# A recurrent layer and a mixture of experts in one pass: visits planned anew, kept rows written later

## The chip, the cores and the metric

The kernel runs on one core of a Trainium2 chip. The metric is the device time of one execution in microseconds, as the median of several runs; lower is better. The engines are PE (matrix multiply), DVE (vector), ACT (scalar), POOL (GpSimd) and SP (sync, which here only reads a few registers and issues transfers).

## The reference

`x` and `f_logit` are 4 x 5056 x 256. A gated recurrence runs over the 5056 steps, and its output passes through a layer of 8 experts, of which each token uses at most one.

```python
def _attn_ref(x, f_logit, lower_bound):
    sig = 1.0 / (1.0 + np.exp(-f_logit))
    f = lower_bound[None, None, :] + (1.0 - lower_bound[None, None, :]) * sig
    i = 1.0 - f
    for t in range(S):
        h = f[:, t] * h + i[:, t] * x[:, t]
        y[:, t] = h
...
def _moe_ref(x, w_skip, w_gate, w1, w2):        # x: 20224 x 256
    do_compute = x @ w_skip > 0
    out = x.copy()
    xc = x[do_compute]
    logits = xc @ w_gate
    e_idx = np.argmax(logits, axis=1)
    ...
    gate_w = probs[np.arange(len(xc)), e_idx]
    for e in range(E):                           # E = 8, hidden width 1024
        mask = e_idx == e
        h = np.maximum(xc[mask] @ w1[e], 0.0)
        y[mask] = gate_w[mask, None] * (h @ w2[e])
    out[do_compute] = xc + y
```

On the reference's inputs 9914 of the 20224 tokens are computed, between 937 and 1630 for each expert; the others keep the recurrence's output.

## The kernel before

The sequence is cut into 21 **chunks**: two of 128 steps, eighteen of 256, one of 192, each for all four batches, so a full chunk has 1024 tokens, eight tiles of 128. A chunk goes through these steps:

- `load_z`, `load_x`: two transfers of 1 MB, issued by ACT (`zt` has two buffers, `xt` three).
- `tanh`, `affine` on ACT, `mixin`, `carry_in` and four `scan` on DVE: the recurrence.
- `turn_out`: for each tile PE transposes the states and computes the nine scores; ACT's `evict` brings them to `rows` (three buffers).
- `route0` to `route3`, `exps`, `gates`: on DVE mostly, with two small matmuls: the expert of each token and its place in a table in memory, ordered by expert.
- `send`: one indirect transfer per tile on POOL writes the token's row to its place in that table (`dispatched`).
- `keep`: one transfer of 1 MB, issued by ACT, writes the recurrence's rows to the output.

A **visit** takes `ns` tiles of one expert's part of the table through both matrix products. `window` (DVE) computes from the counts of chunk `m` which rows it takes; if too few are there, it reaches back over rows that were done, and masks these. `fetch` (SP) reads the rows once all sends of chunks up to `m` have landed. `load_w` (SP) brings the weights in four pieces of 512 KB; each is split into a high half on ACT (`split_hi`) and a low one on DVE (`split_lo`). `turn_in` transposes the rows on PE, `x_hi` and `x_lo` split them. Then come eight blocks of the hidden width (in four steps for `ns` = 2): `first` (three products of halves for each of two depths), `rect_hi` on ACT, `rect_lo` on DVE, `second`. `weigh` (DVE) multiplies by the gate and `put_out` (POOL, one indirect transfer per tile) writes the rows over the kept ones; for that it needs the kept rows of all chunks up to `m`.

`VISITS` lists the fixed visits as (expert, tiles, m). What is left of each expert afterwards is listed on the chip itself, after the last chunk is routed: `list1` to `list4` (some fifty small DVE operations, four transposes and two matmuls) cut the rest into visits of two and three tiles, and the listed visits read their expert and place from that list. `SURE` says how many of these are written out in the program, of two tiles and of three; a loop at the end would run any others.

The **order** of all instructions on each engine is written out before the program is built. Each step is a job with an engine, an estimated cost, a due time and the jobs and buffers that it needs; a greedy simulation gives each engine, whenever it is free, the startable job with the earliest due time. On the chip each engine runs its instructions in that order, and waits on semaphores for what an instruction really needs. A need that stands only in the plan moves an instruction's place in the queue and adds no wait of its own.

Due times come from `begin`, the nominal start of each visit, counted from `T0` = 57 with 5.76 us a tile and 0.47 us a `turn_out`; `ready` of a chunk is the begin of the first visit that needs it, less `FETCH`. A chunk's loads are due at `ready` - 46, its scans at - 24, its sends at - 11, its `keep` at + 4. Fetch and window of a visit are due at its begin - `FETCH`, its weight loads 16 before their use.

Of the kernel before, what the change touches and what calls it, by code (L numbers as in the profile page):

```python
# [36 lines left out]
RW = D + 2  # L37
EW = 2 * E1 + D

T0, FETCH, LAG = 57.0, 22.0, 3  # L40
LOWR = 80

VISITS = [(3, 2, 3), (1, 3, 4), (2, 3, 5), (5, 3, 7), (6, 4, 8), (0, 4, 10), (4, 4, 12), (7, 4, 13), (1, 4, 15),
          (3, 4, 17), (5, 4, 18)]
SURE = ((0, 16), (1, 3))


def tiles_of(c):
    return CHUNKS[c][1] * B // P
# [25 lines left out]
class Plan:  # L75
# [6 lines left out]
    def job(self, eng, cost, due, fn, *args, need=(), takes=(), uses=(), kb=0, lands=2.8):  # L82
        j = Job(eng, cost, due, fn, args, [n for n in need if n is not None], list(takes), kb, lands, len(self.jobs))
        for s_ in list(takes) + list(uses):
            s_.users.append(j)
        self.jobs.append(j)
        return j
# [67 lines left out]
def hgrn_moe(ctx, tc, z_d, x_d, lb_d, wr_d, w1_d, w2_d, out_d, disp_d):  # L155
# [9 lines left out]
    job = plan.job  # L165
# [44 lines left out]
    for nt in sorted({tiles_of(c) for c in range(NCH)}):  # L210
        r = cp.tile([P, E1, nt], F32, name=f"reset{nt}")
# [168 lines left out]
    W1S, W2S = [P, KD, F // 2], [P, NFB // 2, D]  # L380
    NV = len(VISITS)
    mask_all = cp.tile([P, NV, MS], I32, name="mask_all")
    offi_all = cp.tile([P, NV], I32, name="offi_all")
    visits = [dict(e=e, ns=ns, i=i, m=m, w={}, raw={}, hid={}) for i, (e, ns, m) in enumerate(VISITS)]

# [156 lines left out]
    def list2():  # L542
# [6 lines left out]
        for w, (num, frm) in enumerate(tl_["nums"]):  # L549
# [3 lines left out]
            le = new(f"left{w}", [P, 1])  # L553
            V.tensor_scalar(out=le, in0=inc[:, E - 1:E], scalar1=float(-SURE[w][1]), scalar2=0.0,
                            op0=ALU.add, op1=ALU.max)
# [47 lines left out]
    def tail_visit(w, i):  # L603
        ns = 2 + w
        v = dict(ns=ns, tail=True, m=NCH - 1, w={}, raw={}, hid={})

        def mask():
            mk = sb.tile([P, MS], I32, name="mk", bufs=3)
            lim = sb.tile([P, 1], F32, name="lim", bufs=3)
            V.tensor_copy(lim, limr[:, w, bass.ds(i, 1)])  # L610
            V.tensor_scalar(out=mk[:, :ns], in0=seqf[ns], scalar1=lim, scalar2=float(-BIG),
                            op0=ALU.subtract, op1=ALU.mult)
            v["mk"] = mk[:, :ns]

        v["mask"] = mask
        v["off"] = lambda: SP.value_load(lrow[0:1, 2 * w, bass.ds(i, 1)], min_val=0, max_val=ROWS - ns * P)
        v["ereg"] = lambda: SP.value_load(lrow[0:1, 2 * w + 1, bass.ds(i, 1)], min_val=0, max_val=E - 1)
        return v

    sure = [(0, i) for i in range(SURE[0][1])]  # L620
    for i in range(SURE[1][1]):
        sure.insert((i + 1) * len(sure) // (SURE[1][1] + 1), (1, i))
    visits += [tail_visit(w, i) for w, i in sure]
# [6 lines left out]
    PE_TILE, PE_TURN, DVE_CHUNK = 5.76, 0.47, 11.0  # L630
    begin, t, last = [], T0, VISITS[0][2]
    for v in visits:
# [19 lines left out]
    J = {}  # L652
    J["clear"] = job("SP", 1.3, ready[0], clear, kb=660)
    for c in range(NCH):
        nt, r = tiles_of(c), ready[c]
        cols = CHUNKS[c][1] * B
        f = cols / (B * TC)
        s_z, s_x, s_r = new_slot("zt"), new_slot("xt"), new_slot("rows")
        st[c].update(s_x=s_x)
        lz = job("ACT", .66, r - 46, load_z, c, takes=[s_z], kb=cols)  # L660
        lx = job("ACT", .66, r - 45.5, load_x, c, takes=[s_x], kb=cols)
        mix = []
        for k in range(KD):
            t_ = job("ACT", .17 + .86 * f, r - 29 + 2 * k, tanh, c, k, need=[lz], uses=[s_z])
            a_ = job("ACT", .33 + .86 * f, r - 28 + 2 * k, affine, c, k, need=[t_], uses=[s_z])
            mix.append(job("DVE", .13 + 1.08 * f, r - 26 + k, mixin, c, k, need=[a_, lx], uses=[s_z, s_x]))
        ci = job("DVE", .5, r - 24.5, carry_in, c, need=mix + J.get(("scan", c - 1), []),
                 uses=[s_z, s_x] + ([st[c - 1]["s_x"]] if c else []))
        sc = [job("DVE", .06 + 1.08 * f, r - 24 + i, scan, c, i, need=[ci], uses=[s_z, s_x]) for i in range(4)]
        J["scan", c] = sc  # L670
        ev = []
        for j in range(nt):
            s_p = new_slot("pt")
            half = 2 * (j >= nt // 2)
            to = job("PE", PE_TURN, r - 20 + j * 5 / nt, turn_out, c, j, need=sc[half:half + 2], takes=[s_p], uses=[s_x])
            ev.append(job("ACT", .31, r - 19.8 + j * 5 / nt, evict, c, j, need=[to],
                          takes=[s_r] if j == 0 else [], uses=[s_p] + ([s_r] if j else [])))
        J["keep", c] = job("ACT", .62, r + 4, keep, c, need=ev, uses=[s_r], kb=cols)
        r0 = job("DVE", .62, r - 14, route0, c, need=ev + [J.get(("gates", c - 1))], uses=[s_r])
        xp = job("ACT", .25, r - 14, exps, c, need=[r0])  # L680
        r1 = job("DVE", 1.2, r - 14, route1, c, need=[r0])
        s_p, s_o = new_slot("pt"), new_slot("posi")
        r2 = job("PE", .06, r - 13.5, route2, c, need=[r1], takes=[s_p])
        r3 = J["route3", c] = job("DVE", 1.1, r - 13, route3, c, need=[r2], takes=[s_o], uses=[s_p])
        ga = J["gates", c] = job("DVE", .55, r - 13, gates, c, need=[xp, r3], uses=[s_r])
        J["send", c] = [job("POOL", 1.28, r - 11 + j * 1.2, send, c, j, need=[r3, ga], uses=[s_r, s_o], kb=129, lands=4.0)
                        for j in range(nt)]

    l1 = job("DVE", 2.7, begin[len(VISITS)] - FETCH - 12, list1, need=[J["route3", NCH - 1]])
    l2 = job("DVE", 7.0, begin[len(VISITS)] - FETCH - 11, list2, need=[l1])  # L690
    s_p, s_q = new_slot("pt"), new_slot("pt")
    l3 = job("PE", .9, begin[len(VISITS)] - FETCH - 8, list3, need=[l2], takes=[s_p, s_q])
    l4 = job("DVE", 1.0, begin[len(VISITS)] - FETCH - 7, list4, need=[l3], uses=[s_p, s_q])
    win = None
    split_of, fetched = {}, None
    for v, t in zip(visits, begin):
# [10 lines left out]
        else:  # L707
# [5 lines left out]
                           kb=ns * 129, lands=4.5)  # L713
# [14 lines left out]
        for k in range(KD):  # L728
# [3 lines left out]
                     uses=[s_p] + ([s_xh] if k else []))  # L732
            xr.append(job("DVE", .1 + .52 * w, t - 3, x_lo, v, k, need=[xh], takes=[s_xl] if k == 0 else [],
                          uses=[s_p, s_xh] + ([s_xl] if k else [])))
        s_po = [new_slot("po") for _ in range((ns + 1) // 2)]
        sec = None
        for u in range(n):
# [4 lines left out]
                     uses=[s_xh, s_xl] + ws[h, "w1"][1])  # L742
            hi = job("ACT", .1 + .43 * w * nb, tu + .5 * step, rect_hi, v, u, need=[f1], takes=[s_hh], uses=[s_ph])
            lo = job("DVE", .09 + .52 * w * nb, tu + .6 * step, rect_lo, v, u, need=[hi], takes=[s_hl],
                     uses=[s_ph, s_hh])
# [5 lines left out]
        for s_ in range(ns):  # L751
            ob = job("DVE", .42, end - 1, weigh, v, s_, need=[sec, po], takes=[s_ob] if s_ == 0 else [],
                     uses=[s_po[s_ // 2], s_in] + ([s_ob] if s_ else []))
            job("POOL", 1.36, end + 1 + s_, put_out, v, s_, need=[ob] + [J["keep", c] for c in range(m + 1)],
                uses=[s_ob, s_in], kb=128)
# [6 lines left out]
    with tc.If(more > 0):  # L762
        for w in range(2):
            cnt = nc.values_load(Tn[0:1, 1 + w:2 + w], min_val=0, max_val=P)
            with tc.If(cnt > SURE[w][1]):
                with tc.For_i(SURE[w][1], cnt, 1) as ri:
                    v = tail_visit(w, ri)
# [61 lines left out]
```

## Time and profile before

| | |
|---|---|
| median of 3 runs | 658.42 us (656.15 to 659.28) |
| the profiled execution | 660.33 us |
| its span, first to last instruction | 658.6 us |
| mean granted PE clock | 0.936 |
| first matmul of a visit | 97.0 us |
| last matmul of a visit | 651.1 us |

The profile shows one execution. Its times run from the first instruction, in us unless marked ns. "PEclk" is the share of its clock that PE was granted. "A<-B" behind an idle time names what ended it. In a group, the numbers behind the bar are the busy time and the mean duration of one; a tile name without its number stands for all its buffers. PE's matmuls are pipelined, so their rows overlap, and the step from one start to the next is the better price.

### The profile page before, as it was taken

To read this page: it belongs to the slowest core of one execution; us is meant where nothing else is said; L and a number is where in the kernel's file an instruction comes from. 1 tells how busy PE (TensorE), PEld (TensorE's weight loads), DVE (VectorE), ACT (ScalarE), POOL (GpSimd) and SP (SyncE) were. 2 spreads that over 40 slices of the span, in tenths; PEclk is the share of its full clock that TensorE was granted. 3 is DMA by queue.
4 is the path that set the end of the run, shared out by engine and by line. 5 is a ranking of instruction groups with operands and counts; after the bars stand their busy time and mean duration, and the time that the engine had idled before them with its cause. 6 is when DMAs were issued, how large, how long until landed. Compare 5 with 4: busy or idle time off the path is not lost. (4 is left out here: it accounts for less than half of the span.)

```text
span 658.6 us, 12335 instructions
## 1 busy us (share of the span) xinstructions
PE 585.1 (89%) x4202; PEld 555.3 (84%) x4202; DVE 531.4 (81%) x1190; ACT 379.9 (58%) x616; POOL 294.0 (45%) x271
## 2 busy tenths in 40 slices
PE   3356449999999998999999979999999999999995
PEld 3255449998989897979897969999999999999995
DVE  6878788999999997999999686877688677867762
ACT  4564557866776757567665415565556555545540
POOL 1427772685748745867756750411131122111212
PEclk9566669999999997999999979999999999999999
DMA  8989885988978877989756437676567558656710
GB/s 295 417 281 293 289 288 202 302 261 310 339 267 283 312 251 260 320 281 313 274 177 229 140 103 267 204 256 223 164 204 232 171 169 276 208 176 198 246 60 31
DMA packets 61413, 157.59 MB, mean 239 GB/s; under 512 B 9577, under 2 KB 30849, under 8 KB 56736
## 3 DMA queue, kind: packets, MB, share of 16 engines
q1 hardware_dynamic: 22544, 74.16, 35.0%
q10 hardware_dynamic: 27376, 62.13, 27.7%
q0 software_dynamic: 11424, 20.44, 8.5%
q8 instruction: 35, 0.57, 0.4%
q14 instruction: 34, 0.28, 0.1%
HBM read 114.91 MB, written 52.73 MB: 255 GB/s over the span
## 5 line engine op out<-in xcount | busy, mean ns | idle before, releaser
L374 POOL DMA_INDIRECT dispatched<-rows,posi x158 | 202.0, 1279 | 101.2 <-issue 27.7
L514 POOL DMA_INDIRECT out<-ob,xin x80 | 88.7, 1109 | 254.3 <-DVE ob L510 208.3
L481 ACT ACTIVATE hh<-ph 128x512 fp32r<-128x512 f32 (+1 forms) x172 | 97.5, 567 | 161.6 <-PE ph L474 158.5
L503 PE MATMUL po<-w2h,hh 128*128 128x256 f32 x640 | 185.6, 290 | 0.0
L503 PE MATMUL po<-w2h,hl 128*128 128x256 f32 x640 | 180.1, 281 | 0.0
L503 PE MATMUL po<-w2l,hh 128*128 128x256 f32 x640 | 180.0, 281 | 0.0
L488 DVE SCALAR_TENSOR_TENSOR hl<-ph,hh 128x512 fp32r<-128x512 f32 (+1 forms) x172 | 110.9, 647 | 61.2 <-ACT hh L481 60.7
L474 PE MATMUL ph<-xh,w1h 128*128 128x256 f32 (+2 forms) x480 | 157.0, 327 | 0.0
L474 PE MATMUL ph<-xl,w1h 128*128 128x256 f32 (+2 forms) x480 | 154.8, 323 | 0.0
L474 PE MATMUL ph<-xh,w1l 128*128 128x256 f32 (+2 forms) x480 | 154.4, 322 | 0.0
L292 PE MATMUL pt<-rk,xt 128*128 128x137 f32 x632 | 110.6, 324 | 39.3 <-DVE xt L285 18.0
L292 PEld LDWEIGHTS pt<-rk,xt 128*128 128x128 f32 x632 | 98.4, 222 | 49.0 <-DVE xt L285 19.4
L503 PEld LDWEIGHTS po<-w2h,hl 128*128 128x128 f32 x640 | 121.2, 189 | 1.2
L503 PEld LDWEIGHTS po<-w2h,hh 128*128 128x128 f32 x640 | 120.8, 189 | 1.0
L503 PEld LDWEIGHTS po<-w2l,hh 128*128 128x128 f32 x640 | 121.0, 189 | 0.0
L474 PEld LDWEIGHTS ph<-xl,w1h 128*128 128x128 f32 x480 | 91.7, 191 | 5.1
L474 PEld LDWEIGHTS ph<-xh,w1h 128*128 128x128 f32 x480 | 92.1, 192 | 3.3
L474 PEld LDWEIGHTS ph<-xh,w1l 128*128 128x128 f32 x480 | 91.8, 191 | 3.4
L285 DVE TENSOR_TENSOR_SCAN xt<-zt,xt 128x512 f32<-128x512 f32 (+2 forms) x84 | 93.6, 1146 | 0.2
L298 ACT ACTIVATE rows<-pt 128x274 f32<-128x274 f32 x158 | 62.2, 398 | 48.6 <-PE pt L292 43.2
L431 DVE TENSOR_TENSOR w1l<-rw,w1h 128x1024 fp32r<-128x1024 f32 x60 | 73.2, 1220 | 10.1 <-ACT w1h L426 9.7
L431 DVE TENSOR_TENSOR w2l<-rw,w2h 128x1024 fp32r<-128x1024 f32 x60 | 73.2, 1220 | 7.9 <-ACT w2h L426 7.9
(116 smaller groups left out, 541.5 us busy)
## 6 DMA issues: line engine op xcount, KB each, us to landing
rw<-w SPq DMA_DIRECT2D x120, 512.0 KB, 4.6
xt<-x ACTq DMA_DIRECT2D x18, 1024.0 KB, 7.2
zt<-z ACTq DMA_DIRECT2D x18, 1024.0 KB, 8.2
out<-rows ACTq DMA_DIRECT2D x18, 1024.0 KB, 9.1
xin<-dispatched SPq DMA_DIRECT2D x17, 258.0 KB, 3.8
xin<-dispatched SPq DMA_DIRECT2D x7, 516.0 KB, 3.6
dispatched<-rows,posi POOLq DMA_INDIRECT x158, 5.0
xin<-dispatched SPq DMA_DIRECT2D x6, 387.0 KB, 5.3
```

Source lines behind the costliest of these rows:

```text
L285: V.tensor_tensor_scan(out=xt[:, k, sl], data0=zt[:, k, sl], data1=xt[:, k, sl], initial=0.0, op0=ALU.mult, op1=ALU.subtract)
L292: T.matmul(pt[:, k * (E1 + P):(k + 1) * (E1 + P)], xt[:, k, cs], rk[k], start=True, stop=True)
L298: A.activation(st[c]["rows"][:, j], st[c]["pt", j], AF.Copy)
L374: si = G.indirect_dma_start(out=disp_d, out_offset=bass.IndirectOffsetOnAxis(ap=posi[:, j:j + 1], axis=0), in_=rows[:, j, E1:E1 + RW], in_ ...
L431: V.tensor_tensor(out=lo, in0=v["raw"][h, nm], in1=v["w"][nm, h][0], op=ALU.subtract)
L474: T.matmul(ph[:, i], a[:, k, cs], b[:, k, :w], start=(n == 0), stop=(n == 5))
L481: A.activation(th, v["hid"][u], AF.Relu)
L488: V.scalar_tensor_tensor(out=tl, in0=ph, scalar=0.0, in1=th, op0=ALU.max, op1=ALU.subtract)
L503: T.matmul(po, a[:, i, cs], b[:, c], start=(fb == 0 and n == 0 and s % 2 == 0), stop=(fb == NFB - 1 and n == 2), skip_group_check=True)
L514: oi = G.indirect_dma_start(out=out_d, out_offset=bass.IndirectOffsetOnAxis(ap=v["ids"][:, s, D:D + 1], axis=0), in_=v["ob"][:, s], in_off ...
```

## The change

The list of fixed visits is new: 20 instead of 11, with 70 tiles instead of 39. The first four have two tiles and ask for one chunk more each; then, with two exceptions of three tiles, all have four. The last four ask for the last chunk. The listed visits written out go from 16 of two tiles and 3 of three to 2 and 2. `FETCH` goes from 22 to 30. In the plan, `keep` of a chunk needs the first scan of the chunk two later.

```diff
-T0, FETCH, LAG = 57.0, 22.0, 3
+T0, FETCH, LAG = 57.0, 30.0, 3
 LOWR = 80
 
-VISITS = [(3, 2, 3), (1, 3, 4), (2, 3, 5), (5, 3, 7), (6, 4, 8), (0, 4, 10), (4, 4, 12), (7, 4, 13), (1, 4, 15),
-          (3, 4, 17), (5, 4, 18)]
-SURE = ((0, 16), (1, 3))
+VISITS = [(3, 2, 3), (1, 2, 4), (2, 2, 5), (5, 2, 6), (0, 3, 7), (6, 4, 8), (1, 3, 9), (4, 4, 10), (7, 4, 11),
+          (3, 4, 12), (5, 4, 13), (6, 4, 14), (1, 4, 16), (2, 4, 17), (0, 4, 18), (4, 4, 19), (5, 4, 20),
+          (1, 4, 20), (3, 4, 20), (7, 4, 20)]
+SURE = ((0, 2), (1, 2))
...
-        J["keep", c] = job("ACT", .62, r + 4, keep, c, need=ev, uses=[s_r], kb=cols)
+        if c >= 2:
+            J["keep", c - 2].need.append(sc[0])
+        J["keep", c] = job("ACT", .62, r + 4, keep, c, need=ev + [], uses=[s_r], kb=cols)
```

## The prediction

> **What bounds the kernel now.** I read the page first (share of each engine, then the 40 slices), then busy time by stretch, then the timelines around the first visit, the middle and the token list.
>
> ```profile
> span 658.6 us, 12335 instructions
> PE 585.1 (89%) x4202; PEld 555.3 (84%) x4202; DVE 531.4 (81%) x1190; ACT 379.9 (58%) x616; POOL 294.0 (45%) x271
> PE   3356449999999998999999979999999999999995
> PEclk9566669999999997999999979999999999999999
> ```
>
> The shares hide stages. In the first six slices (to 99 us) PE is half idle at a clock near 0.6; then it is nearly full to the end, with small dents.
>
> ```profile
> 0.00:97.00 97.00, 44.86 (x189) 38.74 (x189) 73.90 (x234) 54.10 (x89) 49.56 (x69) 0.66 0.91 310
> 97.00:150.00 53.00, 52.98 (x395) 52.42 (x395) 48.04 (x105) 39.11 (x69) 29.89 (x26) 0.97 0.79 262
> 150.00:200.00 50.00, 48.47 (x341) 45.07 (x341) 46.81 (x109) 35.70 (x63) 32.32 (x26) 1.00 0.86 297
> 200.00:250.00 50.00, 46.49 (x328) 42.51 (x327) 47.06 (x103) 33.39 (x54) 33.12 (x27) 1.00 0.85 292
> 250.00:300.00 50.00, 47.79 (x301) 42.53 (x300) 45.26 (x102) 32.16 (x55) 34.59 (x29) 0.93 0.83 280
> 300.00:350.00 50.00, 47.34 (x333) 43.09 (x332) 47.65 (x104) 33.86 (x56) 32.59 (x25) 1.00 0.79 261
> 350.00:379.00 29.00, 28.93 (x195) 26.19 (x195) 23.17 (x62) 12.12 (x25) 22.75 (x19) 1.00 0.50 165
> 379.00:393.00 14.00, 10.05 (x45) 7.83 (x44) 12.69 (x73) 2.39 (x4) 8.56 (x9) 0.77 0.22 67
> 393.00:651.00 258.00, 258.00 (x2094) 256.89 (x2093) 185.91 (x307) 137.05 (x206) 48.66 (x45) 1.00 0.61 199
> ```
>
> The columns are stretch, length, busy PE, PEld, DVE, ACT, POOL, then clock, DMA share, GB/s. So there are four stages. To 97 us no visit runs. From 97 to 150 PE is full. From 150 to 350 PE idles 1.53 + 3.51 + 2.21 + 2.66 = 9.9 us while DVE is busy 186.8 of 200. From 379 to 393 it idles 3.95 us beside the list of the tail. From 393 to 651 it has no gap at all, on a DVE 72% busy. Only what stands before 393 can be won.
>
> **PE's own prices** (chain of waits of a 2-tile visit, then a pair of turn-outs):
>
> ```profile
> 623.32 0.44 PE px L438 x4
> 623.76 1.43 PE po L503 x12
> 625.19 1.41 PE ph L474 x12
> 234.97 1.10 PE L292 MATMUL pt<-rk,xt 128*128 128x137 f32 x8
> 235.81 0.49 PE L474 MATMUL ph<-xh,w1h 128*128 128x512 f32 x1
> ```
>
> A 2-tile visit is 4 x (1.43 + 1.41) + 0.44 = 11.8 us, 5.9 a tile. A 4-tile visit has the same columns per tile, so 23.6. Two turn-outs take 235.81 - 234.97 = 0.84 us and delay the next matmul a little: 0.47 each with that, 3.8 per chunk of eight.
>
> **The change part by part.**
>
> *The tiles.* Before: 39 tiles in 11 fixed visits and 41 in 19 listed ones. After: 70 in 20 and 10 in 4. Both make 80. Counting the reference's own tokens by expert and chunk, the rows that overlap at the ends of windows rise from 59 to 182, and what is left needs just the 2 + 2 listed visits, so the loop behind them runs for neither kernel. PE's matmul work is the same: 0.
>
> *Six visits fewer* (30 to 24) remove 24 weight loads of 512 KB, 24 high splits on ACT and 24 low splits on DVE (1.2 us each, rows below). All are missing after 393, where PE has 258.00 of 258.00 us and DVE 185.91: worth 0. Nine more windows (five small DVE operations each, under 1 us together) replace fifteen masks: 0, covered by the same room on DVE.
>
> *The middle* is the largest term.
>
> ```profile
> 218.97 0.48 PE L474 MATMUL ph<-xh,w1h 128*128 128x512 f32 x1
> 377.48 0.48 PE L474 MATMUL ph<-xh,w1h 128*128 128x512 f32 x1
> L285 DVE TENSOR_TENSOR_SCAN xt<-zt,xt 128x512 f32<-128x512 f32 x42 | 49.4, 1209 | 0.0
> L488 DVE SCALAR_TENSOR_TENSOR hl<-ph,hh 128x512 fp32r<-128x512 f32 (+1 forms) x51 | 33.0, 650 | 3.0 <-ACT hh L481 2.6
> L431 DVE TENSOR_TENSOR w1l<-rw,w1h 128x1024 fp32r<-128x1024 f32 x13 | 15.8, 1213 | 0.0
> L431 DVE TENSOR_TENSOR w2l<-rw,w2h 128x1024 fp32r<-128x1024 f32 x12 | 14.6, 1219 | 0.0
> L510 DVE SCALAR_TENSOR_TENSOR ob<-po,xin 128x256 f32<-128x256 f32 x24 | 10.6, 474 | 0.0
> ```
>
> The first two rows are the first matmuls of the sixth and the eleventh visit: 158.5 us for five visits, 31.7 each. PE's need per visit there is 23.6 + 62/5 turn-outs x 0.47 = 29.4. The groups are DVE's from 150 to 350: 42 scans are 10.5 chunks, 51 low halves 6.4 visits. The visit rows sum to 33.0 + 15.8 + 14.6 + 10.6 = 74.0, 11.7 a visit; the other 112.8 of 186.8 give 10.7 a chunk. The old plan asks for ten chunks in six visits: 1.67 x 10.7 + 11.7 = 29.6 of 31.7 us, 93%: DVE is the bound. The new plan asks about one chunk per 4-tile visit from chunk 8 on: 10.7 + 11.7 = 22.4 on DVE (24 with the small operations that I booked on chunks) against 23.6 + 3.8 = 27.4 on PE. PE becomes the bound, DVE stands at 82 to 88%. The dents cost 9.9 us idle and one stretch at half clock:
>
> ```profile
> 252.64 0.79 PE L474 MATMUL ph<-xh,w1h 128*128 128x512 f32 x1
> 256.99 0.40 PE L474 MATMUL ph<-xh,w1l 128*128 128x512 f32 x1
> ```
>
> Ten matmuls in 4.35 us, where ten at full clock take 2.4 (twice 1.43 / 12 each, for twice the columns): 2.0 lost. Together 11.9; bounds 0 (the chunks crowd as before) and -12; I take -10, for DVE stays above 80% in a fixed order.
>
> *The list.* It now runs far ahead of the tail, with fixed visits still to do.
>
> ```profile
> 379.64 0.18 DVE halves L532
> 387.64 0.58 PE ltp L593 x2
> ```
>
> Eight microseconds of DVE in one piece, and PE's queue stops at its transposes. The 3.95 us idle and some 2 us at half clock are 6. The block itself stays, so bounds are 0 and -6; I take -4, since the next visit's weights no longer wait for it.
>
> *Kept rows and FETCH.* The first visit's path:
>
> ```profile
> 49.81 1.13 POOL L374 DMA_INDIRECT dispatched<-rows,posi  x1 [12.31 <-ACT rows L298]
> 8.38 45.56 SPq L421 DMA_DIRECT2D rw<-w  x10
> 79.37 13.96 SPq L407 DMA_DIRECT2D xin<-dispatched  x2
> xin<-dispatched SPq DMA_DIRECT2D x17, 258.0 KB, 3.8
> 90.67 0.80 PE L292 MATMUL pt<-rk,xt 128*128 128x137 f32 x2 [3.82 <-ACT zt L260]
> 93.27 1.38 PE L438 MATMUL px<-ident,xin 128*128 128x128 f32 x4
> 96.99 0.58 PE L474 MATMUL ph<-xh,w1h 128*128 128x256 f32 x1
> 14.75 0.62 ACTq L368 DMA_DIRECT2D out<-rows  x1
> 21.38 0.58 ACTq L368 DMA_DIRECT2D out<-rows  x1
> 32.27 2.00 ACT L260 ACTIVATE zt<-zt 128x1024 f32<-128x1024 f32 x2 [4.94 <-DMA zt<-z]
> 16.50:33.00 16.50, 5.05 (x20) 4.05 (x20) 13.52 (x40) 9.44 (x14) 7.07 (x6) 0.54 1.03 419
> ```
>
> Sends of chunk 2 begin at 49.81 on POOL, those of chunk 3 follow, and the first of the two fetches in the SP row goes at 79.37. ACT had stood 4.94 us on the z of chunk 3, with the evictions of chunk 2 behind it, while the DMA engines were full at 419 GB/s. The kept rows of chunks 0 and 1 (1.05 MB) were issued at 14.75 and 21.38; held back, they free 1.05 MB / 419 GB/s = 2.5 us for that z. Bounds 0 and -4.94; I take -2.5. The price is that a buffer of `rows` (three) is free later: a kept row now waits in ACT's order until two chunks on, and the eviction three chunks on needs it written. That leaves the write one chunk's time; should it miss that, evictions and with them PE's turn-outs wait. Behind POOL's sends, `put_out` needs kept rows up to its m; the visit between covers that. FETCH moves windows, fetches (SP) and all chunk rows 8 us ahead of weight loads and visit rows; SP's weight loads can queue behind a fetch whose sends are late. Ten loads (two and a half visits) were issued by 54 us, before the first fetch, so I book 0.
>
> *The early visits.* Up to chunk 8 both plans run 11 tiles, the new one in five visits, not four: one more set of splits (4 x 1.2 on DVE) and 2 MB. PE was full from 97 to 150 at DVE 91%, so cover is thin: 0 to +22 (rival 2); I take +2, nearest to the row of 97 to 150.
>
> **Sum.** -10 - 4 - 2.5 + 2 = -14.5: a span of 644.1. The profiled execution took 660.33, its span 658.6; it lies 1.9 above the median 658.42 of the runs. So 645.8 for such a profile, 643.9 for a median: 644.
>
> **Rivals.**
>
> 1. *The first visit moves by more.* A fetch of this size lands 3.8 us after its issue, so at 83.2, ten before the transposes at 93.27. PE's queue held them behind turn-outs of chunk 6 (row at 90.67), which waited for their scan. With the transposes ahead of these, visits start up to 9 us sooner: 635, and 630 if the dents go entirely. For it: due times of both move. Against: chunk rows move ahead, not behind. It works the other way too.
>
> 2. *The early visits starve, slower.* One chunk per 2-tile visit asks DVE for 10.7 + 4 x 0.65 + 4 x 1.2 + 2 x 0.47 = 19.1 us, PE for 15.6. Without reserve that is 3.5 a visit, and a wait costs 2.0 more at half clock: four visits, 22 us instead of my 2: 664. It decides above 4 us a visit. For it: the early stretch moves 310 GB/s, and each visit brings 2 MB. Against: PE's row at 90.67 already turns out chunk 6, when the second and third visits need chunks 4 and 5, and ten weight loads are done; and from 97 to 150 PE is full.
> The row of 250 to 300 shows the clock at 0.93 after such a wait. The Trainium skill ("TensorE: Matmul & The Clock Gate", "HAM oscillation") says that a wait longer than one activity window sets the array back to half rate, every time; by that rule four waits cost 8 us more than the waits. The trace agrees in its one case here (2.0 us).
>
> 3. *The change doesn't thin the middle.* The order is written greedily, so chunks may run ahead whenever DVE has a gap, as crowded as now until their buffers are full. Then only the list and the start gain: 654. For it: nothing but `rows` holds a chunk back. Against: on an engine the earlier due goes first, and by the code's own arithmetic chunks from 8 on are mostly due 22 to 28 us apart, not 16.
>
> **How the numbers follow.** My forecast 0.52 (637 to 651), rival 1 0.20, rival 3 0.15, rival 2 0.13. Half a percent (3.3 us) is about what a measurement of this kernel can tell from no change. Faster: forecast, rival 1 and most of rival 3, 0.81; same: 0.08; slower: 0.11. The range 630 to 657 leaves out rival 2 and the far end of rival 1.
>
> **What the profile after would show.** Right: PE idle under 3 us per 200 us once 4-tile visits run, their first matmuls 27 to 28 us apart; DVE under 90% there; the list under a running visit; 96 weight loads; first `ph` near 94. Wrong: first `ph` after 100; waits with clock 0.5 among the first five visits; `rows` evictions waiting for a DMA of kept rows; the last chunk sent as early as 380.

## The result and the profile after

| | before | after |
|---|---|---|
| median beside each other, 4 runs each | 657.28 us (655.46 to 659.28) | 634.4 us (632.86 to 635.67) |
| ratio | | 0.965 (0.9608 to 0.9692) |
| the profiled execution, its span | 660.33, 658.6 us | 632.86, 631.1 us |
| first matmul of a visit | 97.0 us | 91.1 us |
| last matmul of a visit | 651.1 us | 624.1 us |

The medians are 22.9 us apart, the two profiled executions 27.5: the one before lies 3.1 us above its median, the one after 1.5 below. Eight of the twelve experiments fell on another chip, on which the kernel before took 696 to 697 us and PE, DVE and ACT now and then stood still together; their totals are set only against each other. Further down, medians from there are over all runs and ratios over the fast ones alone; the profiles of only the visits, of only the hold and of the old visits with a fixed tail are of slow runs, and the other five by themselves bear out what is said of PE's idle time.

The page of the kernel after, its first lines, and the weight loads from its part on DMA issues:

```profile
span 631.1 us, 11424 instructions
PE 572.8 (91%) x3914; PEld 530.4 (84%) x3914; DVE 500.7 (79%) x1159; ACT 355.0 (56%) x576; POOL 299.8 (48%) x271
PE   3275569998999999999999999999999999999995
PEclk9667869999999999999999999999999999999998
rw<-w SPq DMA_DIRECT2D x96, 512.0 KB, 4.9
```

Behind the start, PE's row has one 8 left where it had an 8 and a 7, and the two 7s in the clock's row are gone; 96 weight loads are left. Busy time by stretch of the kernel after, with the columns as before:

```profile
0.00:97.00 97.00, 49.15 (x233) 42.22 (x234) 80.23 (x242) 57.28 (x96) 55.17 (x73) 0.75 0.91 314
97.00:150.00 53.00, 52.93 (x449) 52.26 (x448) 48.85 (x120) 40.75 (x66) 31.99 (x26) 1.00 0.81 268
150.00:200.00 50.00, 48.25 (x337) 45.20 (x336) 47.17 (x101) 34.31 (x58) 29.47 (x24) 1.00 0.88 302
200.00:250.00 50.00, 49.96 (x352) 47.07 (x352) 46.92 (x101) 33.19 (x54) 28.80 (x22) 1.00 0.90 308
250.00:300.00 50.00, 50.00 (x338) 45.52 (x337) 47.30 (x101) 33.12 (x53) 28.07 (x23) 1.00 0.81 286
300.00:350.00 50.00, 49.92 (x347) 45.56 (x346) 47.34 (x94) 34.68 (x58) 37.95 (x30) 1.00 0.80 270
350.00:379.00 29.00, 28.98 (x201) 26.47 (x200) 27.23 (x61) 17.43 (x31) 18.03 (x14) 1.00 0.73 256
379.00:393.00 14.00, 14.00 (x99) 12.72 (x98) 11.58 (x29) 5.46 (x9) 7.71 (x7) 1.00 0.61 190
393.00:624.00 231.00, 229.61 (x1575) 213.39 (x1573) 143.18 (x316) 98.82 (x154) 60.68 (x56) 1.00 0.42 137
```

From 150 to 350 PE idles 1.75 + 0.04 + 0.00 + 0.08 = 1.9 us instead of 9.9. From 379 to 393 it idles nothing instead of 3.95; the 1.39 us missing in the last row are the list's, which now runs later. DVE is as busy as before: 188.7 of 200 from 150 to 350, where it was 186.8. What it does has changed, as the groups of DVE in that stretch, after, show:

```profile
L286 DVE TENSOR_TENSOR_SCAN xt<-zt,xt 128x512 f32<-128x512 f32 x39 | 46.5, 1211 | 0.0
L489 DVE SCALAR_TENSOR_TENSOR hl<-ph,hh 128x512 fp32r<-128x512 f32 (+1 forms) x60 | 38.4, 645 | 5.5 <-ACT hh L482 5.0
```

39 scans for 42 and 60 low halves for 51: 9.8 chunks and 7.5 visits in 200 us, where it was 10.5 and 6.4. The time per visit is what the first matmuls of the ninth and the seventeenth visit say (timeline of PE, after):

```profile
249.55 0.39 PE L475 MATMUL ph<-xh,w1h 128*128 128x512 f32 x1
471.33 0.41 PE L475 MATMUL ph<-xh,w1h 128*128 128x512 f32 x1
```

221.8 / 8 = 27.7 us, against 31.7 before. The list, from timelines of POOL, DVE and PE after:

```profile
441.64 0.97 POOL L375 DMA_INDIRECT dispatched<-rows,posi  x1 [0.30 <-issue]
443.85 1.22 DVE L432 TENSOR_TENSOR w1l<-rw,w1h 128x1024 fp32r<-128x1024 f32 x1
445.12 0.17 DVE L552 TENSOR_TENSOR_SCAN inc<-onesE,whole 128x8 f32<-128x8 f32 x1
451.54 0.38 PE L594 MATMUL ltp<-ident,lf 128*1 128x128 f32 x2 [0.97 <-DVE lf L577]
```

The last chunk's sends end at 442.6 (before, at 387.3). PE waits 0.97 us for the list's block on DVE, inside a visit's stream. And the start, from timelines of ACT's queue, ACT, POOL, SP's queue and PE:

```profile
30.28 0.62 ACTq L369 DMA_DIRECT2D out<-rows  x1
29.19 1.06 ACT L261 ACTIVATE zt<-zt 128x1024 f32<-128x1024 f32 x1 [2.17 <-DMA zt<-z]
46.33 1.13 POOL L375 DMA_INDIRECT dispatched<-rows,posi  x1 [8.79 <-ACT rows L299]
75.53 26.01 SPq L408 DMA_DIRECT2D xin<-dispatched  x3
82.33 0.80 PE L293 MATMUL pt<-rk,xt 128*128 128x137 f32 x2 [3.70 <-ACT zt L261]
87.45 1.11 PE L439 MATMUL px<-ident,xin 128*128 128x128 f32 x4
91.06 0.37 PE L475 MATMUL ph<-xh,w1h 128*128 128x256 f32 x1
```

The first kept rows go at 30.28 instead of 14.75. The wait for the z of chunk 3 falls from 4.94 to 2.17 us and ends at 29.2 instead of 32.3; the sends of chunk 2 begin 3.5 us sooner, the first fetch 3.8, PE's wait in the turn-outs of chunk 6 ends 8.3 sooner (82.33 for 90.67), the transposes begin 5.8 and the first visit 5.9 sooner.

**Where the 27.1 us to the last matmul come from.** Start: 5.9. Idle time of PE from 150 to 350: 9.9 - 1.9 = 8.0. The list: 3.95 - 1.39 = 2.6. Two stretches at half clock before, which the same stretch after doesn't have:

```profile
250.00:257.00 7.00, 6.44 (x22) 5.12 (x21) 5.06 (x16) 5.06 (x7) 2.87 (x3) 0.51 1.01 352
386.60:393.40 6.80, 5.75 (x20) 4.67 (x21) 6.59 (x25) 0.60 (x1) 3.60 (x4) 0.50 0.33 91
```

```profile
250.00:257.00 7.00, 7.00 (x45) 6.28 (x44) 6.59 (x11) 4.61 (x8) 5.78 (x5) 1.00 0.91 336
```

(The first two rows are of before, the third of after.) PE was busy for 6.44 and 5.75 us of them, so half rate cost at most 3.2 and 2.9, together 6.1. With the other three that is 22.6 at most. The other 4.5 or more lie in PE's busy time, and were not divided further.

### The profile page after: what moved, and what is told of

Same layout as the page of the kernel before. It is cut to its first block, busy times and chain, and to the rows that moved or that the text cites. A ratio compares the mean times of both kernels' runs of the same rounds, so it can differ in the third digit from the quotient of the medians.

```text
span 631.1 us, 11424 instructions
## 1 busy us (share of the span) xinstructions
PE 572.8 (91%) x3914; PEld 530.4 (84%) x3914; DVE 500.7 (79%) x1159; ACT 355.0 (56%) x576; POOL 299.8 (48%) x271
## 4 chain that ended last, share of the span: by engine, by line
PE 74%; issue 5%; DVE 5%; ACT 1%; POOL 1%; DMA 0%; POOLq 0%; ACTq 0%; DVEq 0%
PE ph L475 32%; PE po L504 31%; PE pt L293 9%; PE px L439 2%; POOL out L515 1%; DVE xt L286 1%; DVE hl L489 1%; ACT zt L265 1%; DMA dispatched<-rows,posi 0%; DVE w2l L432 0%; DVE xl L452 0%; ACT hh L482 0%; ACT rows L299 0%; DVE xt L269 0%; DVE w1l L432 0%
## 5 line engine op out<-in xcount | busy, mean ns | idle before, releaser
L515 POOL DMA_INDIRECT out<-ob,xin x80 | 95.2, 1190 | 165.0 <-DVE ob L511 145.0
L475 PE MATMUL ph<-xh,w1h 128*128 128x512 f32 (+2 forms) x384 | 140.6, 366 | 0.1
L475 PE MATMUL ph<-xl,w1h 128*128 128x512 f32 (+2 forms) x384 | 137.2, 357 | 0.0
L475 PE MATMUL ph<-xh,w1l 128*128 128x512 f32 (+2 forms) x384 | 137.2, 357 | 0.0
L293 PE MATMUL pt<-rk,xt 128*128 128x137 f32 x632 | 107.6, 316 | 30.5 <-DVE xt L286 16.9
L475 PEld LDWEIGHTS ph<-xl,w1h 128*128 128x128 f32 x384 | 72.6, 189 | 9.4
L475 PEld LDWEIGHTS ph<-xh,w1h 128*128 128x128 f32 x384 | 72.7, 189 | 5.8 <-DVE hl L489 0.3
L475 PEld LDWEIGHTS ph<-xh,w1l 128*128 128x128 f32 x384 | 72.8, 189 | 5.5
L432 DVE TENSOR_TENSOR w2l<-rw,w2h 128x1024 fp32r<-128x1024 f32 x48 | 58.4, 1216 | 8.4 <-ACT w2h L427 8.3
L432 DVE TENSOR_TENSOR w1l<-rw,w1h 128x1024 fp32r<-128x1024 f32 x48 | 58.5, 1219 | 5.9 <-ACT w1h L427 5.8
```

What stands on the lines that cost most here:

```text
L293: T.matmul(pt[:, k * (E1 + P):(k + 1) * (E1 + P)], xt[:, k, cs], rk[k], start=True, stop=True)
L432: V.tensor_tensor(out=lo, in0=v["raw"][h, nm], in1=v["w"][nm, h][0], op=ALU.subtract)
L475: T.matmul(ph[:, i], a[:, k, cs], b[:, k, :w], start=(n == 0), stop=(n == 5))
L515: oi = G.indirect_dma_start(out=out_d, out_offset=bass.IndirectOffsetOnAxis(ap=v["ids"][:, s, D:D + 1], axis=0), in_=v["ob"][:, s], in_off ...
```

## The experiments

**The theory** was that two parts bring the gain: chunks are asked for one visit apart, so that PE no longer waits for DVE in the middle; and the held kept rows let the first visit start sooner. The rivals: that the fixed tail alone (list under a running visit, fewer visits) brings it; that `FETCH` does; that the hold does nothing or does it all.

The first eight runs take the parts one at a time, first from the side of before, then from the side of after.

*Only the visits* (`FETCH` 22, no hold):

```diff
-VISITS = [(3, 2, 3), (1, 3, 4), (2, 3, 5), (5, 3, 7), (6, 4, 8), (0, 4, 10), (4, 4, 12), (7, 4, 13), (1, 4, 15),
...
-SURE = ((0, 16), (1, 3))
+VISITS = [(3, 2, 3), (1, 2, 4), (2, 2, 5), (5, 2, 6), (0, 3, 7), (6, 4, 8), (1, 3, 9), (4, 4, 10), (7, 4, 11),
...
+SURE = ((0, 2), (1, 2))
```

> Only the new visits; FETCH back at 22 and no kept row held back. Theory A (the visits' list thins the chunks to one per 4-tile visit, so that PE no longer waits for DVE, and takes the token list off PE's path; the start is the kept rows' doing): 15 to 17 us below the kernel before, so about 641, with PE's idle time between 150 and 350 us under 3 us and the first matmul of a visit still near 97. Rival B (the visits alone don't do it; the earlier due times of chunks, FETCH, are what keeps PE fed): less than 8 us below, 650 or more, with PE idle 6 us or more between 150 and 350.

*Only the hold* (`FETCH` 22, visits of before):

```diff
+        if c >= 2:
+            J["keep", c - 2].need.append(sc[0])
```

> Only the kept rows held back two chunks; visits and FETCH of before. Theory A: the first matmul of a visit comes 3 to 6 us sooner (91 to 94), and most of that is lost again in the middle, where DVE is the bound and paces the visits by the chunks; the total falls by as much as the chunks come sooner, 2 to 6 us: 652 to 655. Rival C (the start moves by the order of PE's queue, not by free DMA time): first matmul stays within 1 us of 97 and the time within 0.3% of before.

*Only `FETCH`*:

```diff
-T0, FETCH, LAG = 57.0, 22.0, 3
+T0, FETCH, LAG = 57.0, 30.0, 3
```

> Only FETCH 30; visits and kept rows of before. Theory A: nothing, within 0.5% of before (654 to 661), since an earlier due time of all chunks changes few places in the queues. Rival B: 4 us or more below before, with PE idle in the middle falling from 9.9 us.

*The old eleven visits with a fixed tail* behind them, `FETCH` 22, no hold:

```diff
-          (3, 4, 17), (5, 4, 18)]
-SURE = ((0, 16), (1, 3))
+          (3, 4, 17), (5, 4, 18), (1, 4, 20), (2, 4, 20), (3, 4, 20), (4, 4, 20), (6, 4, 20), (7, 4, 20), (0, 3, 20), (5, 3, 20)]
+SURE = ((0, 4), (1, 1))
```

> The first eleven visits of before with their chunks, and behind them eight more fixed visits that ask for the last chunk, so that the token list stands far from the tail; 24 visits as in the changed kernel; FETCH 22, no kept row held back. It parts the token list from the spacing of the chunks. Theory A: only the list's share is won, 4 to 6 us: 651 to 653, with PE idle between 150 and 350 still 8 us or more. Rival D (the fixed tail and six visits fewer are the whole of the gain, by less work for DVE, ACT and the DMA engines at the end): 12 us or more below before, 645 or less.

*After without the hold*:

```diff
-        if c >= 2:
-            J["keep", c - 2].need.append(sc[0])
```

> The changed kernel with the kept rows written as soon as they can be (new visits, FETCH 30). Theory A (the held rows free the DMA engines for the first loads and so move the first visit, by some 6 us, and a PE-bound middle keeps that): 4 to 7 us slower than the changed kernel, that is 0.971 to 0.977 of before, with the first matmul of a visit at 95 to 98. Rival C (the start moves with FETCH or the visits' order, the held rows do nothing): within 2 us of the changed kernel, 0.962 to 0.968.

*After with `FETCH` 22*:

```diff
-T0, FETCH, LAG = 57.0, 30.0, 3
+T0, FETCH, LAG = 57.0, 22.0, 3
```

> The changed kernel with FETCH back at 22 (new visits, kept rows held). Theory A: FETCH is worth nothing or little, 0 to 2 us: 0.962 to 0.969 of before, first matmul of a visit within 2 us of 91. Rival B (the earlier due times keep PE fed): 5 us or more slower than the changed kernel, 0.973 or more, with PE idle time over 5 us between 150 and 350 us.

*After with the visits of before* (`FETCH` 30 and the hold stay), against after:

```diff
+VISITS = [(3, 2, 3), (1, 3, 4), (2, 3, 5), (5, 3, 7), (6, 4, 8), (0, 4, 10), (4, 4, 12), (7, 4, 13), (1, 4, 15),
+          (3, 4, 17), (5, 4, 18)]
+SURE = ((0, 16), (1, 3))
```

> The old visits with both other parts (FETCH 30, kept rows held): what the change does without its list. Theory A: only the earlier start, 3 to 7 us, and DVE still bound in the middle: 0.989 to 0.996 of before, PE idle 8 us or more between 150 and 350. Rival E (the two small parts are most of the gain): 0.980 or less.

*After with the old eleven visits and the fixed tail* (the list of the fourth run; `FETCH` 30 and the hold stay), against before:

```diff
+T0, FETCH, LAG = 57.0, 30.0, 3
...
+          (3, 4, 17), (5, 4, 18), (1, 4, 20), (2, 4, 20), (3, 4, 20), (4, 4, 20), (6, 4, 20), (7, 4, 20), (0, 3, 20), (5, 3, 20)]
+SURE = ((0, 4), (1, 1))
...
+            J["keep", c - 2].need.append(sc[0])
```

> The first eleven visits of before, with their chunks, then eight fixed visits that ask for the last chunk, and 4 + 1 listed; FETCH 30 and kept rows held as in the changed kernel. It differs from the kernel with old visits by the tail alone, and from the changed kernel by the spacing of the chunks alone. Theory A: tail worth 4 to 6 us, spacing 10 to 12: 0.980 to 0.987 of before, PE idle 8 us or more between 150 and 350. Rival D (the fixed tail is the gain): 0.972 or less, within 4 us of the changed kernel.

What these measured. The idle time of PE is that from 150 to 350 us; "less joint stops" leaves out the time in which DVE and ACT stood too, added up from the instructions of the trace. Where no ratio stands, none is on record.

| run | visits | `FETCH` | hold | first `ph` | PE idle | less joint stops | time, us |
|---|---|---|---|---|---|---|---|
| before, there, 23 runs | old | 22 | no | | | | 696.75 (681.12 to 713.3) |
| only the visits | new | 22 | no | 97.92 | 13.6 | 10.0 | 688.35 (677.14 to 691.34) |
| only the hold | old | 22 | yes | 90.04 | 19.7 | 14.1 | 700.21, ratio 1.0196 (1.0116 to 1.0277) |
| only `FETCH` | old | 30 | no | 95.24 | 19.7 | 15.7 | 697.01, ratio 1.0031 (0.9993 to 1.0069) |
| old, then a fixed tail | old + tail | 22 | no | 94.83 | 24.6 | 19.7 | 697.38, ratio 0.9869 (0.9784 to 0.9953) |
| before, there again, 6 runs | old | 22 | no | | | | 696.59 (683.86 to 716.77) |
| after without hold | new | 30 | no | 97.79 | 7.4 | 5.7 | 676.0 (673.45 to 678.76) |
| after with `FETCH` 22 | new | 22 | yes | 91.39 | 13.3 | 8.9 | 680.47 (678.38 to 682.89) |
| after, old visits | old | 30 | yes | 89.69 | 19.1 | 14.0 | 681.07 (677.08 to 683.07) |
| after, old, then a fixed tail | old + tail | 30 | yes | 91.26 | 23.5 | 14.3 | 683.5 (681.78 to 685.04) |

Two columns sort cleanly. With the hold the first visit starts at 89.7 to 91.4, without it at 94.8 to 97.9. The pairs that differ in the hold alone are 95.24 and 89.69, 97.92 and 91.39: it is worth some 6 us, and rival C falls. `FETCH` alone moves the start by 0.4 us at most, the new list by itself makes it 1.3 to 3.1 us later. How the hold does it shows in the thirteen profiles, of both chips, that leave the turn-outs of chunk 6 in their place: without it ACT waits 4.7 to 5.5 us for the z of chunk 3 and those turn-outs begin at 88.5 to 90.7, with it 0.7 to 2.3 us and 81.3 to 83.2. So the 3 us or so that are gained at that z have become some 7 three chunks on.

With the new list PE's idle time in the middle is 5.7 to 10.0 us (mean 8.2), with the old spacing 14.1 to 19.7 (mean 15.6), whatever is done to the tail. The difference is 7.4; between the two kernels themselves, on the other chip, it was 8.0. One row of each kind, busy time from 150 to 350, first of after without hold, then of after with the old visits:

```profile
150.00:350.00 200.00, 192.59 (x1341) 178.05 (x1340) 180.88 (x382) 130.23 (x214) 109.75 (x87) 1.00 0.79 274
```

```profile
150.00:350.00 200.00, 180.87 (x1167) 161.56 (x1166) 165.75 (x364) 120.69 (x203) 128.81 (x99) 0.95 0.74 252
```

Beside the hold and `FETCH` the fixed tail brings nothing: 683.5 with it, 681.07 without. In total time the parts are less plain. `FETCH` alone changes nothing that can be told. The hold alone came out 2% above before by its ratio and half a percent by the medians, although its first visit starts sooner; the fixed tail alone came out 1.3% below by its ratio and level by the medians. The kernel after had its lowest time there without the hold. After with `FETCH` 22 and after with the old visits came to 0.977 and 0.978 of the median of before, which is where rivals B and E had them and not where theory A had; but the six times of before go from 683.86 to 716.77, so this decides nothing.

Rival B has more for it than that. With the new list PE's idle time in the middle is 10.0 and 8.9 us with `FETCH` 22, and 5.7 with 30; theory A had expected under 3 for only the visits, rival B 6 or more there and over 5 in after with `FETCH` 22. Counted in the same way from the first visit's first matmul to the last visit's last, it is 24.0 and 24.5 us with `FETCH` 22, 13.7 with 30, and 26.4 to 32.7 in the five with the old spacing. So on that chip the new list with `FETCH` 22 took away some 40% of the waits in the middle, but less than a fifth over the whole run; the one run with `FETCH` 30 as well took away half. How much of the gain needs the two together stays open.

A joint stop shows how far that chip's totals can be trusted (after without hold, one stretch):

```profile
127.00:135.00 8.00, 0.14 (x2) 0.00 (x0) 0.00 (x0) 0.26 (x2) 6.17 (x7) 0.64 0.43 146
```

For eight microseconds PE, DVE and ACT do next to nothing, and no semaphore in the trace says why. The kernel after itself wasn't run on that chip. What the hold is worth at the end of the kernel stays open; that it moves the first visit is shown.

The last four ran on a chip with the kernel before at 656.22 us (653.9 to 658.07, 11 runs). There theory A says that PE is the bound behind the start, with room on DVE.

*The kernel after once more*, as the measure for the other three:

> The changed kernel itself, beside the others of this call and of the two calls before, whose chip ran the kernel before at 697 us. Theory A: 20 to 30 us below before on this chip too, so 667 to 677; 0 to 3 us below it without held rows would mean that the held rows are worth nothing there. First matmul of a visit at 91.

635.08 us (633.77 to 635.47), ratio 0.9676 (0.9651 to 0.97); first `ph` at 91.23; PE idle 3.0 us from 150 to 350. The result holds. Its early stretch is less full than in the first profile: PE idles 4.1 us from 97 to 200 instead of 1.8, and the sixth visit begins at 175.4 instead of 174.7.

*Transposes of the first visit ahead of the turn-outs of chunk 6*, a need in the plan alone:

```diff
+            J["to", c, j] = to
...
+            if v is visits[0]:
+                for j in range(8):
+                    J["to", 6, j].need.append(ti)
```

> The changed kernel with one need more in the plan: the turn-outs of chunk 6 come behind the first visit's input transposes on PE. Nothing is left out. Theory A (PE is the bound from the first visit to the last, so any earlier start is kept to the end): first matmul of a visit at 84 to 87 instead of 91, and 3 to 6 us below the changed kernel. Rival F (the start is not the bound: chunks 6 and 7 come later by as much and the early visits wait for them): first matmul earlier, but the time within 2 us of the changed kernel or above it.

637.75 us (635.5 to 638.29), ratio 0.9709 (0.9682 to 0.9736). From timelines of PE, ACT and DVE of this kernel:

```profile
79.66 0.55 PE L439 MATMUL px<-ident,xin 128*128 128x128 f32 x2 [0.57 <-DMA xin<-dispatched]
83.19 2.35 ACT L265 ACTIVATE zt<-zt,fa,fc 128x1024 f32<-128x1024 f32 x2
85.46 0.63 ACT L446 ACTIVATE xh<-px 128x256 fp32r<-128x256 f32 x2
83.00 3.45 DVE L286 TENSOR_TENSOR_SCAN xt<-zt,xt 128x512 f32<-128x512 f32 x3
88.12 0.75 DVE L452 TENSOR_TENSOR xl<-px,xh 128x256 fp32r<-128x256 f32 x2
88.59 4.93 PE L293 MATMUL pt<-rk,xt 128*128 128x137 f32 x20 [7.19 <-DVE xl L452]
93.16 0.51 PE L475 MATMUL ph<-xh,w1h 128*128 128x256 f32 x1
```

Against the kernel after beside it the transposes run 8.0 us sooner (79.66 for 87.62), and the first visit starts 1.9 us later. `x_hi` waits on ACT behind the affine step of chunk 7, `x_lo` on DVE behind scans; PE, whose queue is in a fixed order, stands 7.19 us. Time stayed within what rival F expected, but not for its reason: since the start didn't come sooner, whether a sooner start would be kept wasn't tested.

*The low split of `w1` done twice*, and told to the plan (the output is the same; 48 operations more):

```diff
-        V.tensor_tensor(out=lo, in0=v["raw"][h, nm], in1=v["w"][nm, h][0], op=ALU.subtract)
+        for _ in range(2 if nm == "w1" else 1):
+            V.tensor_tensor(out=lo, in0=v["raw"][h, nm], in1=v["w"][nm, h][0], op=ALU.subtract)
...
-                lo = job("DVE", 1.21, use - 4, split_lo, v, h, nm, need=[hi], takes=[s_lo], uses=[s_raw, s_hi])
+                lo = job("DVE", 2.42 if nm == "w1" else 1.21, use - 4, split_lo, v, h, nm, need=[hi], takes=[s_lo], uses=[s_raw, s_hi])
```

> The changed kernel with the low split of the first weights done twice (same values), 1.2 us more on DVE for each of 48 pieces, 2.4 us per visit, told to the plan. Theory A (DVE, though busy 94% in the middle of the changed kernel, fills its gaps with chunks that are not needed yet; PE is the bound, with 3 us to spare per chunk and 4-tile visit): 0 to 8 us above the changed kernel. Rival G (a DVE 94% busy is the bound or next to it): the whole of it on the path while chunks run, 16 visits x 2.4 = 38 us, or at least half, 19 us above.

650.21 us (648.27 to 651.86), ratio 0.9914 (0.9888 to 0.9939): 15.1 us more for 48 x 1.2 = 58 us of DVE work. Theory A said at most 8, rival G at least 19: neither holds as it stood. Busy time by stretch, first of this kernel, then of the kernel after run beside it:

```profile
97.00:200.00 103.00, 93.56 (x700) 88.55 (x699) 95.56 (x204) 67.76 (x112) 49.29 (x43) 0.98 0.76 264
200.00:400.00 200.00, 195.61 (x1322) 177.97 (x1321) 189.52 (x384) 123.99 (x204) 108.54 (x91) 0.99 0.73 257
```

```profile
97.00:200.00 103.00, 98.93 (x759) 94.69 (x759) 93.96 (x216) 73.21 (x121) 59.10 (x48) 1.00 0.81 280
200.00:400.00 200.00, 199.86 (x1374) 183.79 (x1375) 186.37 (x391) 127.40 (x210) 125.87 (x97) 1.00 0.79 272
```

PE loses 5.4 us up to 200 and 4.3 more up to 400. By the first matmuls of visits, the five from the first (90.7, beside it 91.2) to the sixth (182.7, 175.4) lose 8.0 of the 12 us that they were given; the eleven from the sixth to the seventeenth (486.1, 472.9) lose 5.8 of 26, half a microsecond each. So DVE has little room under the small early visits, and later takes up nearly four fifths of the extra work. Where that room lies, the scans of the last chunk and the first matmul of the visit that needs it show, first in the kernel after run beside it, then in this kernel (from timelines of DVE and PE):

```profile
377.51 0.95 DVE L286 TENSOR_TENSOR_SCAN xt<-zt,xt 128x384 f32<-128x384 f32 x1
472.87 0.41 PE L475 MATMUL ph<-xh,w1h 128*128 128x512 f32 x1
```

```profile
430.70 2.65 DVE L286 TENSOR_TENSOR_SCAN xt<-zt,xt 128x384 f32<-128x384 f32 x3
486.07 0.48 PE L476 MATMUL ph<-xh,w1h 128*128 128x512 f32 x1
```

The kernel after scans chunk 9 55.2 us before the visit that needs it and the last one 95.4 us before; with the extra work these are 56.8 and 55.4. So part of what keeps DVE busy in the kernel after is work done ever further ahead, and this is what gave way.

*Three tiles from the second visit on* instead of two, the rest of the list spaced as in after:

```diff
-VISITS = [(3, 2, 3), (1, 2, 4), (2, 2, 5), (5, 2, 6), (0, 3, 7), (6, 4, 8), (1, 3, 9), (4, 4, 10), (7, 4, 11),
...
-SURE = ((0, 2), (1, 2))
+VISITS = [(3, 2, 3), (1, 3, 4), (2, 3, 5), (5, 3, 7), (6, 4, 8), (0, 3, 9), (4, 4, 10), (7, 4, 11), (3, 4, 12), (5, 3, 13),
+          (6, 4, 14), (1, 4, 16), (2, 4, 17), (0, 4, 18), (4, 4, 19), (5, 4, 20), (1, 4, 20), (3, 4, 20), (7, 4, 20)]
+SURE = ((0, 4), (1, 1))
```

> The changed kernel with the first visits of before (2, 3, 3, 3 tiles for chunks 3, 4, 5, 7, then 4 for chunk 8) in front of the new spacing; 19 fixed visits, 4 + 1 listed, 24 in all, 80 tiles; FETCH 30 and held rows as in the changed kernel. Theory A (the spacing of the later chunks is what counts, the small first visits cost or bring little): within 4 us of the changed kernel. Rival H (starting with small visits keeps PE fed early): 6 us or more above it.

631.61 us (630.11 to 633.26), ratio 0.963 (0.9603 to 0.9657), 3.5 below the kernel after beside it; the two intervals just touch, the times of the runs (up to 633.26, from 633.77) don't. First `ph` at 89.82. Busy time of this kernel:

```profile
97.00:200.00 103.00, 101.91 (x739) 97.91 (x738) 97.23 (x216) 75.49 (x125) 64.55 (x50) 1.00 0.86 293
```

PE idles 1.1 us where the kernel after idled 4.1 in the run beside it (1.8 in its first profile). Theory A stands, with up to 4 us for the small first visits; rival H, which had this kernel 6 us slower, falls. This is the fastest version that was run.

## Why the prediction was right, and where its sizes were off

It said 644 (630 to 657), and 634.4 came out: the direction and the range held. The forecast's own part of it, 637 to 651, did not: its sum of 14.5 us fell 8.4 short of the 22.9 between the medians. Its steps:

- **The middle, -10: right in kind.** 8.0 us idle and up to 3.2 at half clock are 11.2, inside its bound of 12. How much of it the list of visits brings without `FETCH` 30 is open. PE idles under 3 us in 200, and visits come 27.7 us apart for the 27.4 of its arithmetic.
- **DVE at 82 to 88%, under 90%: wrong.** It is at 94%, 93 before. The prediction put one chunk to a visit; from 150 to 350 there were 9.8 chunks to 7.5 visits, 1.3 to one, and at its own prices that is 1.3 x 10.7 + 11.7 = 25.6 of 27.7 us. Rival 3 had the reason: chunks run ahead wherever DVE has a gap; the last one is scanned 95 us before its visit. But it drew the wrong end from that (654): the chunks done ahead hardly make PE wait here. The Trainium skill ("Perfetto Trace Analysis", "Identifying the Most-Contended Engine") takes the occupancy of the vector engine as a fair measure of how near it is to its limit. In these traces it did not tell whether DVE holds PE back: at 93 and 94% PE's idle time was 9.9 and 1.9 us, and with 58 us of work more DVE's busy time from 200 to 400 rose by just 3.2.
- **The list, -4.** 2.6 idle and up to 2.9 at half clock are 5.5, inside its bound of 6. It does run under a visit.
- **Kept rows, -2.5: the term that was mis-sized most, 5.9 measured.** The prediction priced one wait, that for the z of chunk 3. It did fall by 2.8 us. The term left out what rival 1 names: the first transposes stand in PE's order behind turn-outs of chunk 6. What is gained at the z of chunk 3 grows on the way there: 3.1 us at that z, 3.8 at the fetch, 8.3 at the turn-outs of chunk 6, and likewise in every run with the hold. The bound of 4.94 was the length of that one wait, and so too short.
- **Early visits, +2: right in sign, covered in the sum.** PE was full from 97 to 150 in the first profile and idled 1.2 us there in the second. Bigger first visits save 3.5 us, so the small ones do cost about that. Nothing near the 22 of rival 2.
- **`FETCH`, 0:** right for `FETCH` alone, 1.0031 (0.9993 to 1.0069). With the new list it is open: PE idled 8.9 and 10.0 us in the middle with 22 and 5.7 with 30, and the prediction had no term for the two together.
- **Six visits fewer, 0; tiles, 0:** beside the hold and `FETCH` the fixed tail brings nothing (683.5 against 681.07), as the full PE of that stretch had said.
- **First `ph` near 94: 91.1.** Rival 1 gave 635 for a start that moves by more, and that is the time that came out, but not its mechanism: the transposes stand behind turn-outs of chunk 6 after as before, and the one try to put them ahead moved PE's wait to ACT and DVE.
- **The wrong signs** that it listed didn't show: the last chunk is sent at 442.6, and ACT shows no wait of an eviction for the write of kept rows. PE ran at half clock for some 3 us of the first visit (0.66 from 91 to 96), as before (0.52 from 97 to 100), but without a wait in it.

The 4.5 us or more that are left of the profiled pair stand in no term, and 4.6 of its 27.5 are the choice of the two executions.

## What to carry to other kernels

Where an order is planned by due times, look at how many units of the feeder's work the plan asks for per unit of the consumer's: at an equal busy share of the feeder, the mix decided here whether the consumer waited, and a busy share does not tell work that is needed now from work done ahead. A wait at the start of a pipeline is priced by following it through every stage that the first consumer's queue stands behind, not by its own length. A write that nobody reads soon can be held out of the first microseconds, in which the DMA engines are full.

## What the runs showed of the hardware

Half the clock came after short waits close together, not after one long one. PE in the kernel before, ahead of the stretch at half clock that begins at 250.1, and its busy time in the last 3.4 us:

```profile
245.78 1.09 PE L292 MATMUL pt<-rk,xt 128*128 128x137 f32 x8
248.07 0.73 PE L292 MATMUL pt<-rk,xt 128*128 128x137 f32 x4 [1.20 <-ACT rows L298]
249.60 1.57 PE L438 MATMUL px<-ident,xin 128*128 128x128 f32 x8 [0.75 <-ACT rows L298]
246.70:250.10 3.40, 1.46 (x12) 1.16 (x11) 2.63 (x12) 2.84 (x5) 1.49 (x2) 1.00 0.98 347
```

Two waits, the longer 1.20 us; PE was busy 1.46 of 3.40 us. The Trainium skill ("TensorE: Matmul & The Clock Gate", "HAM oscillation") gives the rule as no idle gap of PE above about 3.4 us; this trace shows that gaps well under it can be too much. (Rival 2 of the prediction took this stretch as agreeing with the rule; it does not.) One wait can be enough too: 1.85 us did it in the kernel with the transposes ahead, at 154.9, and 1.73 us in the kernel after, at 152.0, did not.

```profile
154.63 0.70 PE L439 MATMUL px<-ident,xin 128*128 128x128 f32 x3 [1.85 <-ACT rows L299]
152.03 0.73 PE L293 MATMUL pt<-rk,xt 128*128 128x137 f32 x4 [1.73 <-DVE xl L452]
```

All fourteen traces together say what counts. The shortest stretches at half clock last 3.41 us and the others are multiples of it. Cut in steps of 3.41 us back from its end, time at full clock behind the first matmul of a visit (stretches of over 10 us) gives 44 last steps, after which the clock fell, and 2172 others. In 43 of the 44 PE was busy for 52% of the step or less; in 2165 of the 2172 for 50% or more. So it is the busy share of such a step that goes with the fall, not the length of one gap.

One chip was 6% slower with the same kernel (696.75 for 656.22). On it the time from 100 to 620 us in which PE, DVE and ACT stood still at once was 9.8 to 15.6 us in the eight profiles, and at most 0.6 in the six taken elsewhere; the longest such stop lasted 7.7 us. The cause wasn't found.
